# Rows of the strided attention's loads divided at other places, and one weight load divided instead of three

## The chip, the cores and the metric

The kernel runs on one core of one Trainium2 chip. The metric is the device time of one execution in microseconds (us); the median of several runs stands for a kernel. The core has a matrix engine (PE, with its weight loads as PEld), a vector engine (DVE), a scalar engine (ACT), GpSimd (POOL), a sync engine (SP), and sixteen DMA engines that move data between the chip's memory (HBM) and the on-chip memory of 128 partitions (rows). Accumulators lie in PSUM.

## What is computed

Sparse attention, and behind it a mixing layer in the frequency domain:

```
attn: q, k, v (8 batches, 8 heads, 576 positions, 64)
  heads 0-3: a position sees the 32 positions up to itself
  heads 4-7: a position sees earlier positions with the same remainder mod 32
x = attention output as (8, 576, 512)
X = rfft(x over positions), modes 0..63
Yr = Xr @ w_r[m] - Xi @ w_i[m];  Yi = Xr @ w_i[m] + Xi @ w_r[m]   (64 modes, 512 x 512 each)
u = x + irfft(Y);  out = u + relu(u @ w_ch)
```

Inputs are 32-bit. The weights w_r and w_i, 64 matrices of 1 MB each, are by far the most of what is read.

## The kernel before

All inputs are loaded by DMAs that POOL issues, which also make 16-bit numbers of them. POOL issues in program order, so the order of the load calls is the order of the queue.

**Attention, strided heads** (lines 836 to 858). A loop goes over the eight batches. In it `str_scores` and `str_values` work on batch b while `str_front` prepares batch b + 1 by transposing its v, q and k on PE (`str_turn`, line 278; `str_q`, line 262). Each of q, k and v of one batch is a tile of 72 rows (four heads of 18) by 2048 numbers in `ring`, which has twelve places, three for each of four batches. `load_str` (lines 212 to 224) fills them. For batches 0 and 1 it takes 64 rows of one batch at a time (line 222). For an even batch with nb = 2 it takes two batches at once, rows 0 to 63 in one DMA (line 220) and rows 64 to 71 in a second (line 224), for v, then q, then k. These calls come at line 795 for batches 2 and 3, and at line 839 for batches 4 and 5 (issued in the loop at b = 1) and for batches 6 and 7 (at b = 3). With the three of line 224 in the load of batch 0, there are twelve DMAs of 8 rows in all. In memory, a row of a pair of batches is two runs of 2048 numbers, and each run is one DMA packet of 4096 bytes as written.

**Attention, local heads, and the modes** (lines 868 to 888 and 966 to 974). `load_loc` loads 128 rows for each of v, q and k. The modes of one half of the frequencies' input channels are multiplied between the pieces of local attention, those of the other half behind it, with the output projection's preparation in between.

**The weights.** `w_fetch` (lines 159 to 193) loads them in the order of `ORDER`, in tiles numbered i; a tile holds half of one mode's input channels, and one transfer brings a pair of tiles, or four (`QUADS`). Of a transfer the real part goes to partitions 0 to 63 and the imaginary part to 64 to 127, each with a DMA of 64 rows (line 188; line 192 for the last ones, mode by mode). Three real parts, those of the transfers that begin at tiles 64, 84 and 94, are divided by `UNEVEN` into pieces of given numbers of rows, one DMA each (line 185). The weights go round in ten places of `wring` and three guest tiles; `w_fetch` is called when a pair of modes has been multiplied (lines 610 and 657), so POOL waits for PE there.

A tile's semaphore tells when all its DMA has landed, that is, when every DMA engine that took part has written its share. Eight such semaphores go round over POOL's DMAs, so a DMA is issued only when the eighth before it has landed.

**The end** (lines 1134 to 1176). When the last weights have landed, the last two modes are multiplied, and the inverse transform, the projection and the output's rows follow, two batches at a time; SP issues the stores.

Of the kernel before, what the change touches and what calls it, by code (L numbers as in the profile page):

```python
# [56 lines left out]
def kernel(  # L57
# [10 lines left out]
    nc = tc.nc  # L68
# [78 lines left out]
    SPLIT1, SPLIT0 = 56, 48  # L147
    ORDER = [(1, m) for m in range(SPLIT1)] + [(0, m) for m in range(SPLIT0)]
    ORDER += [(1, m) for m in range(SPLIT1, NM)] + [(0, m) for m in range(SPLIT0, NM)]
    UNEVEN = {64: (25, 12, 27), 84: (6, 54, 4), 94: (10, 54)}  # L150
    QUADS = {p for p in range(13, 54) if (p - 13) % 5 in (0, 2)}
    wring = pw.tile([128, 2 * NWBUF, 4, DM], F16, tag="w", bufs=1, name="wring")
    w_tiles = []
# [5 lines left out]
    def w_fetch(n=1):  # L159
        free_pairs[0] += n  # L160
        while len(w_tiles) < 2 * NM:
# [13 lines left out]
            for ri, src in enumerate((moe_w_r, moe_w_i)):  # L175
# [4 lines left out]
                if ri and not m:  # L180
                    dst, rows = dst[:, 1:nm], rows[:, 1:nm]
                if i in UNEVEN and not ri:
                    a = 0
                    for n in UNEVEN[i]:
                        nc.gpsimd.dma_start(dst[a : a + n], rows[a : a + n])
# [24 lines left out]
        return t[:, ds(1152 * vi, 1152)]  # L210

    def load_str(b, nb):
        for vi in (2, 0, 1):
            n = 3 * (b % 4) + SLOT[vi]
            two = ring[:, n : n + 4 : 3, :]
            src = SRC[vi][b - b % 2 : b - b % 2 + 2, 4:8].rearrange(
                "b h (c r) d -> (h c) b (r d)", r=32
            )
            if nb == 2:
                nc.gpsimd.dma_start(two[0:64], src[0:64])  # L220
            else:
                nc.gpsimd.dma_start(ring[0:64, n, :], src[0:64, b % 2])
            if b % 2 == 0:
                nc.gpsimd.dma_start(two[64:72], src[64:72])

    def load_loc(*bs):
        for b in bs:
# [560 lines left out]

    psum_pools(tp=3, sc=3, av=2)
    load_str(0, 1)  # L790
    const_load(nc.scalar, "cI", "cM6", "cM5")
    load_str(1, 1)
    const_load(nc.sync, "cT", "cMl")
    strided_tokens()
    load_str(2, 2)
    w_fetch()

# [212 lines left out]
    for n, i in enumerate([3, 5, 7] + list(range(8, 21))):  # L1010
        b, t = n // 2, n % 2 * 2
# [195 lines left out]
```

## Time and profile before

| what | value |
|---|---|
| median of 3 runs | 423.84 us (423.45 to 425.29) |
| the profiled execution's own time | 423.73 us |
| its span, first to last instruction | 421.7 us |
| PE busy | 327.8 us (78%) |
| DVE, ACT, POOL busy | 236.9, 220.8, 112.2 us (56, 52, 27%) |
| moved by DMA | 91.62 MB in 29914 packets, mean 217 GB/s |
| chain of waits that ended last | DMA 48%, PE 27%, DVE 12%, ACT 6% |

The page of the profile gives the busy time of each engine, the span in 40 equal slices (a digit is the busy share in tenths; for DMA, the mean of the sixteen engines), and the DMA queues with their packets. In the list of the chain of waits, each line has a start, a length and what the time went to; a line of a DMA goes from the end of its issue to its landing. In a timeline, a line has start, length, engine, line of the kernel, operation, output and inputs, shape and count, and in brackets the idle time before it with what ended it. Beneath the page lie the records themselves: every DMA packet with its start, length and size (not with its engine), and for every DMA the sixteen times at which a DMA engine raised its semaphore.

### The profile page before, as it was taken

How to read it: one execution, taken by the hardware profiler on the slowest of the kernel's cores; microseconds unless marked ns; L12 is line 12 of the kernel's file. 1: busy time of each engine (PE TensorE's matmuls, PEld its weight loads, DVE VectorE, ACT ScalarE, POOL GpSimd, SP SyncE). 2: the span in 40 equal slices, each digit the busy share in tenths (PEclk: the TensorE clock that was granted, in tenths of full speed). 3: DMA queues.
4: the chain of work that ended last, by engine and by line, in shares of the span. 5: the costliest groups of instructions: out<-in, count | busy, mean ns of one | idle time of the engine just before them, and what ended most of it. 6: DMA issues, size and time to landing. Idle time of an engine off the chain costs nothing.

```text
span 421.7 us, 9817 instructions
## 1 busy us (share of the span) xinstructions
PE 327.8 (78%) x4156; PEld 201.8 (48%) x4156; DVE 236.9 (56%) x501; ACT 220.8 (52%) x423; POOL 112.2 (27%) x183
## 2 busy tenths in 40 slices
PE   3987878679999198888867858587569748889993
PEld 3866767564656155556534424244235423444320
DVE  3788788950364224555323627756276454665795
ACT  2687778742666157475752513532153345544693
POOL 8332333322422011212031211212112213220594
PEclk9999899956999779899995989999689988999998
DMA  8999999999999999999999999999999999999498
GB/s 149 211 211 212 214 212 213 210 212 210 215 213 213 214 214 214 214 215 214 212 214 214 213 214 214 214 213 213 213 213 215 213 214 214 213 213 182 177 380 341
DMA packets 29914, 91.62 MB, mean 217 GB/s; under 512 B 3952, under 2 KB 4720, under 8 KB 29872
## 3 DMA queue, kind: packets, MB, share of 16 engines
q0 software_dynamic: 24624, 81.28, 97.2%
q1 hardware_dynamic: 4816, 9.65, 6.2%
q8 instruction: 32, 0.52, 0.5%
q10 hardware_dynamic: 432, 0.08, 0.1%
q14 instruction: 10, 0.08, 0.0%
HBM read 162.83 MB, written 9.44 MB: 409 GB/s over the span
## 4 chain that ended last, share of the span: by engine, by line
DMA 48%; PE 27%; DVE 12%; ACT 6%; issue 4%; POOL 1%; DVEq 0%; POOLq 0%; ACTq 0%
DMA wring<-in_moe_w_i_dram 43%; PE y L599 6%; DMA wring<-in_moe_w_r_dram 4%; DVE xb L243 3%; DVE kz L285 3%; PE p L1032 2%; PE sc L534 2%; ACT X L253 2%; PE p L1052 2%; PE sc L461 1%; PE tp L415 1%; ACT PL L491 1%; PE y L534 1%; DVE rec L242 1%; DMA ring<-in_v_dram 1%
## 5 line engine op out<-in xcount | busy, mean ns | idle before, releaser
L599 PE MATMUL y<-wring,X 128*32 128x512 f16 (+1 forms) x424 | 49.1, 454 | 34.5 <-DMA wring<-in_moe_w_i_dram 34.5
L188 POOL DMA_DIRECT2D wring<-in_moe_w_r_dram x39 | 23.7, 607 | 186.4 <-PE y L599 162.5
L253 ACT ACTIVATE yr<-y 128x512 f16<-128x512 f32 x28 | 16.7, 597 | 59.7 <-PE y L599 58.0
L599 PEld LDWEIGHTS <-X 128*32 128x32 f16 (+1 forms) x448 | 21.9, 143 | 48.2 <-DMA wring<-in_moe_w_i_dram 33.0
L751 DVE COPY xo<-tp 128x512 f16<-128x512 f16 x32 | 22.1, 692 | 38.0 <-PE tp L749 38.0
L741 PE MATMUL sc<-w_cp,xT 128*128 128x512 f16 x128 | 37.4, 416 | 1.4 <-DVE xT L709 1.4
L750 ACT ACTIVATE v<-sc 128x512 f16<-128x512 f32 x32 | 19.1, 597 | 36.1 <-PE sc L741 36.1
L243 DVE TENSOR_TENSOR xb<-av,rec 90x256 f16<-90x256 f32 (+2 forms) x80 | 36.0, 450 | 2.7
L491 ACT ACTIVATE PL<-sc 128x480 f16<-128x480 f32 (+1 forms) x48 | 26.9, 578 | 17.2 <-PE sc L477 16.8
L242 DVE RECIPROCAL rec<-av 90x4 f32<-90x4 f32 (+2 forms) x80 | 14.6, 183 | 35.0 <-PE av L506 24.3
L422 DVE COPY qT<-tp 128x576 f16<-128x576 f16 x16 | 11.9, 752 | 37.3 <-PE tp L415 37.3
L1004 DVE TENSOR_TENSOR xo<-p,xo 128x512 f16<-128x512 f32 x32 | 20.6, 686 | 18.2 <-PE p L784 18.2
L188 POOL DMA_DIRECT2D wring<-in_moe_w_i_dram x42 | 25.5, 608 | 9.6 <-DMA wring<-in_moe_w_i_dram 5.3
L380 ACT ACTIVATE PL<-sc 90x360 f16<-90x360 f32 (+1 forms) x48 | 22.8, 490 | 7.0 <-PE sc L373 6.4
L253 ACT ACTIVATE v<-p 128x512 f16<-128x512 f32 x32 | 17.5, 594 | 14.9 <-PE p L784 14.8
L415 PE MATMUL tp<-cI_s,ring 64*64 64x64 f16 x864 | 23.1, 199 | 2.3 <-DVE qT L422 1.7
L253 ACT ACTIVATE v<-tp 128x640 f16<-128x640 f16 (+1 forms) x24 | 19.0, 807 | 10.6 <-PE tp L449 7.9
L461 PE MATMUL sc<-cMl_s,cI_s 128*128 128x480 f16 (+1 forms) x48 | 19.3, 403 | 5.0 <-ACT PL L491 3.4
L415 PEld LDWEIGHTS <-ring 64*64 64x64 f16 x864 | 18.3, 113 | 8.3 <-issue 4.2
L253 ACT ACTIVATE kz<-tp 64x360 f16<-64x360 f16 (+1 forms) x32 | 18.9, 592 | 6.1 <-PE tp L415 5.2
L1090 POOL TENSOR_TENSOR rl<-rl,xo 128x512 f32<-128x512 f32 x15 | 17.1, 1161 | 14.7 <-DVE rl L1083 13.0
L534 PEld LDWEIGHTS <-xb 108*128 108x128 f16 (+2 forms) x176 | 15.4, 106 | 10.8 <-DVE xb L243 6.2
(153 smaller groups left out, 763.1 us busy)
## 6 DMA issues: line engine op xcount, KB each, us to landing
wring<-in_moe_w_r_dram POOLq DMA_DIRECT2D x17, 1024.0 KB, 17.5
wring<-in_moe_w_i_dram POOLq DMA_DIRECT2D x16, 1024.0 KB, 21.8
wring<-in_moe_w_i_dram POOLq DMA_DIRECT2D x24, 512.0 KB, 17.8
wring<-in_moe_w_r_dram POOLq DMA_DIRECT2D x22, 512.0 KB, 14.7
out_dram<-osb SPq DMA_DIRECT2D x18, 256.0 KB, 2.4
out_dram<-osb SPq DMA_DIRECT2D x9, 512.0 KB, 3.3
ring<-in_v_dram POOLq DMA_DIRECT2D x8, 288.0 KB, 13.3
ring<-in_q_dram POOLq DMA_DIRECT2D x8, 288.0 KB, 13.5
```

What stands on the lines that cost most here:

```text
L188: nc.gpsimd.dma_start(dst, rows)
L243: nc.vector.tensor_tensor(out=dst, in0=val.rearrange("p h (q c) -> p h c q", c=4), in1=rec[0:n, 0:pieces] .to_broadcast((n, pieces, 64)) . ...
L253: nc.scalar.activation(out=out, in_=in_, func=ACTF.Copy)
L380: nc.scalar.activation(out=PS[0:n, ds(POFF[t], 4 * n)], in_=scp[0:n, 0 : 4 * n], func=ACTF.Exp, scale=SCALE,)
L415: nc.tensor.transpose(tp[ds(64 * hp, 64), ds(64 * i, 64)], qn[ds(64 * hp, 64), ds(64 * (9 * g + i), 64)], idn[ds(64 * hp, 64), ds(64 * hp, ...
L461: nc.tensor.matmul(scp[:, 0 : n * times].rearrange("p (h x) -> p h x", h=times), idn, mask_rows("cMl", n, times), start=True, stop=False,)
L491: nc.scalar.activation(out=dst, in_=src, func=ACTF.Exp, scale=SCALE)
L534: nc.tensor.matmul(xp[:, ds(192 * cp, 192)].rearrange("p (f m) -> p f m", f=3), xb[b][0:n, base + t, ds(128 * cp, 128)], F[0:n, :, t, :], ...
L599: nc.tensor.matmul(yp[ds(a, 32), :], Xh[half][pr, c].rearrange("p b r (h m) -> p (b r h) m", h=2)[:, :, mm % 32], wt[pr, XC[c], :], start= ...
L741: nc.tensor.matmul(vp, xT[:, ch], w_chs["cp"][:, ch, :], start=(ch == 0), stop=(ch == 3),)
L751: nc.vector.tensor_copy(out=xo.rearrange("p (h q c) -> p h q c", h=2, c=4), in_=tp[:, 0:512].rearrange("p (h c q) -> p h q c", h=2, c=4),)
L1004: nc.vector.tensor_tensor(out=xo[:, j], in0=up[j], in1=xo[:, j], op=AluOp.add)
```

## The change

Two tables of numbers change, and one line uses the new one.

```
-    UNEVEN = {64: (25, 12, 27), 84: (6, 54, 4), 94: (10, 54)}
+    UNEVEN = {64: (3, 40, 21)}
+    CUT = {4: ((54, 18), (20, 52), (24, 48)), 6: ((2, 70), (2, 70), (20, 52))}
...
     def load_str(b, nb):
-        for vi in (2, 0, 1):
+        for j, vi in enumerate((2, 0, 1)):
             n = 3 * (b % 4) + SLOT[vi]
+            cut = CUT[b][j][0] if b in CUT else 64
...
             if nb == 2:
-                nc.gpsimd.dma_start(two[0:64], src[0:64])
+                nc.gpsimd.dma_start(two[0:cut], src[0:cut])
             else:
                 nc.gpsimd.dma_start(ring[0:64, n, :], src[0:64, b % 2])
             if b % 2 == 0:
-                nc.gpsimd.dma_start(two[64:72], src[64:72])
+                nc.gpsimd.dma_start(two[cut:72], src[cut:72])
```

The 72 rows of batches 4 and 5 are divided at row 54 for v, 20 for q and 24 for k, those of batches 6 and 7 at row 2 for v and q and 20 for k; before, all at row 64. Batches 0 to 3 stay as they are. Of the weights, the real part of the transfer at tile 64 goes in pieces of 3, 40 and 21 rows instead of 25, 12 and 27; those at tiles 84 and 94 go in one DMA of 64 rows instead of three and two pieces. The same bytes go to the same places, and POOL issues 152 DMAs instead of 155. The instructions of the other engines, and their order, are the same.

## The prediction

> **What bounds the kernel now.** I read the forty slices first, then the queues, then the end of the chain of waits, and last the trace's single records of DMA packets and landings, which the page only sums up.
>
> ```profile
> DMA  8999999999999999999999999999999999999498
> GB/s 149 211 211 212 214 212 213 210 212 210 215 213 213 214 214 214 214 215 214 212 214 214 213 214 214 214 213 213 213 213 215 213 214 214 213 213 182 177 380 341
> DMA packets 29914, 91.62 MB, mean 217 GB/s; under 512 B 3952, under 2 KB 4720, under 8 KB 29872
> ```
>
> From slice 2 to slice 37 all sixteen DMA engines are busy at one flat rate: loading is the floor from start to 390 us.
>
> ```profile
> q0 software_dynamic: 24624, 81.28, 97.2%
> q1 hardware_dynamic: 4816, 9.65, 6.2%
> q8 instruction: 32, 0.52, 0.5%
> q10 hardware_dynamic: 432, 0.08, 0.1%
> q14 instruction: 10, 0.08, 0.0%
> ```
>
> q0 holds all that POOL issues. q8 is 32 fetches of 16 KB of code; 0.5% of 16 engines' 421.7 us is 33.7 us, so about 1.05 us of one engine each.
>
> ```profile
> 360.96 0.28 issue
> 361.25 19.41 DMA wring<-in_moe_w_i_dram
> 380.66 0.28 issue
> 380.94 9.58 DMA wring<-in_moe_w_i_dram
> 390.52 0.14 issue
> 390.66 0.41 PE y L642 x8
> ```
>
> The last weights land at 390.52; 31.2 us of mixing and output follow, untouched by the change. So the span moves as the last landing does. A transfer has landed only when the slowest of its engines is through: its sixteen landing increments come from 385.44 to 390.52, 5.1 us apart.
>
> **Reading single engines.** On one engine a 4096-byte packet starts 304.5 ns after the one before it, exact to a few ns, and a 4-byte mark (21 ns) ends the engine's part of a transfer. With these steps the records fall into sixteen tracks. On the tracks the pieces of 25, 12 and 27 rows (218 to 220 us) lie so: five engines carry 10 packets of the first, twelve carry 2 of the second, nine carry 6 of the third. One has the first two, four the first and third, five the second and third, six the second alone. So a piece of n rows runs on the largest number up to 16 that divides n, on neighbours, starting behind the last engine of the piece before; 64 rows run on all. The engines left out of a piece get 4-byte fill records, as many as a carrier has packets. That gives 576 fill records here, and 155 POOL transfers x 16 marks + 576 = 3056. The profile's page agrees: 3952 small packets, less 432 of q10 and 464 of q1 (29 transfers x 16).
>
> I number the engines from the one where the count stood at the start; twelve 8-row pieces (96 places) bring it back to 0 before the 25 rows. The code fetches delay eight engines only, 5, 6 and 9 to 14, in that order as far as these groups tell, by about 1.1 us each (one track jumps 1.08 to 1.11 us at each of 332.2, 359.5, 370.2 and 384.6); each has about four by the end. The other eight get none, but the 8 KB fetches of q14 (0.3 to 0.5 us) hit some of 1 to 4.
>
> **The change, step by step.** Bytes are the same; only the engine that carries them changes. Packets of the split transfers (batches 4 to 7 and tiles 64, 84, 94) on each engine, and when its last mark starts, in us; the new end is the old one plus the difference x 0.3045:
>
> | engine | before | after | end before | end after |
> |---|---|---|---|---|
> | 0 | 80 | 86 | 386.67 | 388.50 |
> | 1 to 4 | 84 | 86 | 387.49, 388.44, 388.89, 390.21 | 388.10, 389.05, 389.50, **390.82** |
> | 5, 6 | 76 | 70 | 390.16, 389.49 | 388.33, 387.66 |
> | 7, 8 | 86 | 86 | 388.56, 388.63 | the same |
> | 9 | 76 | 72 | 390.21 | 388.99 |
> | 10, 11 | 72 | 72 | 389.20, 389.06 | the same |
> | 12 | 72 | 70 | 387.84 | 387.23 |
> | 13, 14 | 72 | 70 | 389.48, 389.95 | 388.87, 389.34 |
> | 15 | 72 | 80 | 385.14 | 387.57 |
>
> Three engines tie for last before: 9, 5 and one of 1 to 4, which I call S. The change takes 1.2 and 1.8 us from the first two and gives S two packets more. So the last mark moves from 390.21 to 390.82, **0.61 us later**.
>
> Tiles 84 and 94 lose three POOL issues (8 of L185 become 3, two of L188 come): 3 x 0.6 us on a queue that is 27% busy and waits 162.5 us for PE alone; nothing. No instruction moves past another. Three marks and 32 fill records less: under 0.1 us per engine, taken as nothing.
>
> *S's own stalls* are what the trace does not settle. S loses 0.52 us at 231.4 and again at 344.7, each beside a fetch of q14. If both recur, 390.82. If both fall on engines with room, S ends at 389.77 and the last is about 389.8 (0.4 us earlier than now); with one more, 391.3 (+1.1). I take that they recur, since the instructions around them are the same.
>
> *Earlier arrivals.* The pieces of batches 4 and 5 put 24 packets instead of 18 on engines 0 to 8 by the end of q, so that q lands 1.8 us later on engine 5, which had its fetch at 35.7: about 44.5 instead of 42.73.
>
> ```profile
> 43.39 0.42 PE L262 MATMUL tp<-cI_s,ring 72*128 72x72 f16 x8 [0.84 <-DVE vT L285]
> ```
>
> PE wants it at 43.39, so it waits some 1.1 us. Behind it on PE stand scores and values of batch 3, and the copies of DVE and the exponentials of ACT wait for those: the attention is late by 1.1 us, or by 0 if it catches up. The q of batches 6 and 7, wanted at 61.74, fits within the same delay. What hides it is the full queue. POOL next waits for that work here:
>
> ```profile
> 107.36 0.58 POOL L188 DMA_DIRECT2D wring<-in_moe_w_r_dram  x1 [5.52 <-PE y L599]
> ```
>
> The first packet follows an issue by 1.5 us (1.25 to 2.77 at the start), so it could run at 108.9. S finishes what it has at 111.89, and with 8 packets more at 114.3: 5.4 us of cover. Engines 5, 6 and 12, with 8 packets less, finish near 109.5 and may idle a microsecond; they end 2.5 us or more before S. Cost nothing; without cover, 1 us per 1 us.
>
> [...] From the transfer ahead of the pieces of 25, 12 and 27 rows to the one behind them, the mean landing of the sixteen engines goes from 231.04 to 236.17: 5.13 us for 16 packets on average (4.87 us). So engines left out of a piece do not idle; they go on with what is queued. [...] Taken as if the others idled, the longest parts of all pieces sum to 106 packets after against 108 before, 0.6 us sooner; the landings above disagree with the idling. In the table engines 7 and 15 are not late (388.6 and 385.1). [...]
>
> **Sum.** 423.73 (the profiled execution: span 421.7 and 2.0 around it) + 0.61 = 424.3; the median of the three runs, 423.84, stands 0.1 above that execution. A difference under 0.5% (2.1 us) is what a measurement of this kernel cannot tell from no change.
>
> **Rivals.**
> - *Evener end* (0.28): S's stalls fall elsewhere. Last mark 389.8 to 390.3, time 423.3 to 423.8. For: 9, 5 and 14, the late ones, are all relieved. Against: the fetches come with the program, which is unchanged.
> - *Pieces on the wrong engines* (0.07): slower. If the count stands one or more places off when batch 4 is issued, the extra packets meet engines with fetches. Turning the last column by 1 to 15 places makes the end 2.3 to 4.0 us later than now: 426 to 427.8. It decides from one place on. Against: the six 8-row pieces ahead of it (48 places) are unchanged and bring the count to 0, and this trace shows 0 at 96.
> - *Attention late beyond the cover* (0.02): slower from 5.4 us of delay at 107 on; at 8 us 426.3. The one wait found is 1.1.
> - *Faster by more than 0.5%* (0.03): even sixteen equal ends would come at the mean, 388.71, 1.5 us sooner (0.35%); the rest would have to come from elsewhere.
> - That nothing but total bytes counts (no change, 423.7) lies inside the first.
>
> **Numbers.** Forecast 0.60 (424.1 to 424.9), evener end 0.28, wrong engines 0.07, late attention 0.02, faster 0.03. Within 0.5%: 0.60 + 0.28 = 0.88; slower 0.09; faster 0.03. The range takes in the first two, and 0.3 for the scatter of medians: 423.2 to 425.2.
>
> **What would show it.** POOL transfers 152, small packets 3952 - 48 - 32 = 3872. Last landing 391.1; S last, by 1.3 us over the next; engines 9 and 5 near 389.0 and 388.3. PE waiting for the q load near 43.4. Wrong if another engine is last, if the landing is over 392.6, or if the queue runs empty near 107 us.

## The result and the profile after

The changed kernel takes 438.03 us (median of six runs, 434.84 to 440.62) against 423.7 us before on the same chip: ratio 1.032, interval 1.030 to 1.035. It is slower by 14 us; the forecast was 424.3. Its profiled execution took 434.84 us, with a span of 432.9. It is the quickest of the six, so the trace shows 11.2 of the median's 14.3 us; where the slower runs lose the rest was not traced. The runs scatter more than before (6 us against 2).

The page, as for before (forty slices of 10.8 us; then the packets and the queue that POOL fills):

```profile
DMA  8999999999999999999999999999999999999498
GB/s 153 207 209 179 161 193 145 202 210 209 211 212 212 207 215 214 213 215 217 212 200 215 212 213 215 214 214 215 213 214 215 213 215 213 213 213 189 155 380 340
DMA packets 29834, 91.62 MB, mean 212 GB/s; under 512 B 3872, under 2 KB 4640, under 8 KB 29792
q0 software_dynamic: 24544, 81.28, 98.4%
```

The DMA engines are as busy as before, 9 tenths in nearly every slice of the loading, but from slice 4 to slice 7 they move less: 145 to 193 GB/s where before had 212 to 214. Packets and bytes are as counted beforehand. So the engines do not wait; each packet takes longer. The busy times by stretch show where. Columns: stretch, length, busy us of PE, its weight loads, DVE, ACT and POOL (with instructions), granted clock, DMA share, GB/s. First before, then after:

```profile
38.00:50.00 12.00, 9.87 (x159) 8.43 (x157) 8.93 (x26) 8.94 (x19) 4.05 (x7) 0.86 1.07 213
60.00:76.00 16.00, 13.08 (x237) 11.10 (x234) 13.18 (x37) 12.61 (x29) 5.56 (x10) 1.00 1.07 212
100.00:390.00 290.00, 226.78 (x2765) 131.12 (x2764) 142.47 (x276) 137.98 (x255) 55.15 (x95) 0.91 1.06 213
```

```profile
38.00:50.00 12.00, 5.10 (x69) 4.09 (x68) 5.35 (x13) 4.17 (x10) 2.52 (x5) 0.64 1.19 136
60.00:76.00 16.00, 11.13 (x162) 9.67 (x163) 9.31 (x28) 8.82 (x21) 3.75 (x8) 0.79 1.18 155
100.00:390.00 290.00, 223.76 (x2696) 130.16 (x2691) 138.64 (x271) 137.00 (x254) 55.26 (x97) 0.90 1.07 213
```

The two bad stretches are those of the newly cut rows, batches 4 and 5, then 6 and 7. In the packet records, 4096-byte packets that start between 38 and 50 us took 512 ns in the median, 86% of them over 400; before, 324 ns and 0.3%. (324 ns is the length of a packet's record; an engine's next packet starts 304.5 ns after the one before, so the records overlap a little.) Between 50 and 58 us, when weights pass, the median is 324 again. The last increments of single transfers tell how much is lost by when:

| transfer, its last landing | before | after | later by |
|---|---|---|---|
| last weights ahead of batch 4 | 37.04 | 37.18 | 0.1 |
| k of batches 4 and 5, second piece | 45.63 | 51.96 | 6.3 |
| k of batches 6 and 7, second piece | 63.56 | 75.18 | 11.6 |
| the local k rows that landed at 86 us | 86.08 | 97.05 | 11.0 |
| last weights | 390.52 | 401.68 | 11.2 |

All is lost by 75 us, and nothing more of note afterwards. The chain of waits says so too (start, length, what); its last line is the last landing, and the 31.2 us behind it are as before:

```profile
17.70 14.65 DMA wt<-in_moe_w_i_dram
32.63 19.32 DMA ring<-in_k_dram
52.25 18.52 DMA ring<-in_q_dram
...
392.06 9.62 DMA wring<-in_moe_w_i_dram
```

PE, which in this stretch of before waited mostly for DVE and ACT, now waits for loads. Of what ended PE's waits from 36 to 80 us, this is the top (us in total, times, longest), first before, then after:

```profile
PE av L394 <- ACT PL L380: 3.0, 9, 0.5
PE tp L262 <- DVE vT L285: 1.7, 2, 0.8
```

```profile
PE tp L264 <- DMA ring<-in_q_dram: 6.7, 2, 3.4
PE tp L280 <- DMA ring<-in_v_dram: 3.1, 1, 3.1
```

### The profile page after: what moved, and what is told of

The parts are those of the page before. It is cut to its first block, busy times and chain, and to the rows that moved or that the text cites. A ratio compares the mean times of both kernels' runs of the same rounds, so it can differ in the third digit from the quotient of the medians.

```text
span 432.9 us, 9812 instructions
## 1 busy us (share of the span) xinstructions
PE 329.9 (76%) x4156; PEld 204.4 (47%) x4156; DVE 237.0 (55%) x501; ACT 221.1 (51%) x423; POOL 110.4 (26%) x180
## 2 busy tenths in 40 slices
DMA packets 29834, 91.62 MB, mean 212 GB/s; under 512 B 3872, under 2 KB 4640, under 8 KB 29792
## 3 DMA queue, kind: packets, MB, share of 16 engines
q0 software_dynamic: 24544, 81.28, 98.4%
## 4 chain that ended last, share of the span: by engine, by line
DMA 58%; PE 26%; DVE 7%; ACT 4%; issue 2%; POOL 1%; DVEq 0%; ACTq 0%; POOLq 0%
DMA wring<-in_moe_w_i_dram 43%; PE y L601 7%; DMA ring<-in_k_dram 4%; DMA ring<-in_q_dram 4%; DMA wt<-in_moe_w_i_dram 3%; DMA ring<-in_v_dram 3%; PE tp L417 2%; PE sc L463 2%; PE p L1034 2%; PE y L536 2%; PE p L1054 2%; DVE xb L245 2%; ACT X L255 1%; PE sc L479 1%; ACT PL L493 1%
## 5 line engine op out<-in xcount | busy, mean ns | idle before, releaser
L189 POOL DMA_DIRECT2D wring<-in_moe_w_r_dram x41 | 24.9, 607 | 204.9 <-PE y L601 178.7
L601 PE MATMUL y<-wring,X 128*32 128x512 f16 (+1 forms) x424 | 48.0, 442 | 37.0 <-DMA wring<-in_moe_w_i_dram 36.5
L255 ACT ACTIVATE v<-tp 128x640 f16<-128x640 f16 (+1 forms) x24 | 19.1, 807 | 10.8 <-PE tp L451 7.7
L280 PE MATMUL tp<-cI_s,ring 72*128 72x72 f16 x256 | 15.8, 210 | 7.0 <-DMA ring<-in_v_dram 5.6
```

The costliest lines, as they stand in the source:

```text
L189: nc.gpsimd.dma_start(dst, rows)
L255: nc.scalar.activation(out=out, in_=in_, func=ACTF.Copy)
L601: nc.tensor.matmul(yp[ds(a, 32), :], Xh[half][pr, c].rearrange("p b r (h m) -> p (b r h) m", h=2)[:, :, mm % 32], wt[pr, XC[c], :], start= ...
```

## The experiments

Two theories of why packets got slower. **P**: engines that write at the same time into the same few partitions hold each other up; before, every 64-row transfer would give engine e the rows 4e to 4e+3, whatever the tensor. (The records do not tell which partition a packet goes to; that an engine's rows are neighbours, in the engines' order, is the author's assumption.) **H**: the conflict is in the reading. Rivals of both: the late weight pieces, engines out of step as such, the number of cuts. All compare with before on the same chip.

**1. The late weight pieces alone.**

```
-    CUT = {4: ((54, 18), (20, 52), (24, 48)), 6: ((2, 70), (2, 70), (20, 52))}
+    CUT = {}
```

> The change's other half alone: tile 64's real part in pieces of 3, 40 and 21 rows, tiles 84 and 94 in one transfer each, and all strided rows cut at 64 of 72 as before. Theory A, that the packets of the new strided pieces are slow by themselves (half of those between 38 and 50 us and between 62 and 73 us of the changed kernel took 500 ns or more, where before nearly all took 324): strided loads as before, last landing within 2 us of 390.5, 422 to 426 us, and no packet median over 330 ns between 24 and 80 us. Theory B, that the late weight pieces cost the time: 434 to 440 us.

424.52 us, ratio 1.0014 (1.0005 to 1.0024); last landing 391.03. From 24 to 80 us no slice of its 40 falls below 203 GB/s. So the weight pieces cost 0.6 us, and the rest comes with the strided cuts.

**2 and 3. Batches 4 and 5 alone, batches 6 and 7 alone** (weight pieces as before).

```
+    CUT = {4: ((54, 18), (20, 52), (24, 48))}
...
+    CUT = {6: ((2, 70), (2, 70), (20, 52))}
```

> Only batches 4 and 5 cut at the new rows (54/18, 20/52, 24/48); batches 6 and 7 at 64, weight pieces as before. Theory A: slow packets between 38 and 50 us as in the changed kernel, about 6 us of its 11.2, thus 428 to 432 us, and the rows of batches 6 and 7 at 324 ns again. Theory C, that engines out of step with each other make every strided transfer slow, cut anew or not: batches 6 and 7, which follow engines that are still 4 us apart, are slow too, 433 us or more.

> Only batches 6 and 7 cut at the new rows (2/70, 2/70, 20/52); batches 4 and 5 at 64, weight pieces as before. Theory A: slow packets only from the second piece of 2 rows on, about 5 us lost, 427 to 431 us. If slow packets need what batch 4 left behind (theory C): batches 6 and 7 run mostly at 324 ns and the time is 424 to 426 us.

439.58 us (ratio 1.034, 1.029 to 1.040) and 431.36 (1.017, 1.015 to 1.019). Each is slower than before, and they do not add: the first alone is as slow as both. In the first, packets took 491 ns in the median from 38 to 50 us. The strided rows of batches 6 and 7, cut at 64 there, came mostly at full rate, with one stretch at 58 us down to 162 GB/s; but from 70 to 84 us, where local rows and weights alternate and engines were over 5 us apart, it falls to 148 to 183 GB/s in four slices of 2 us. From 24 to 104 us, in such slices:

```profile
GB/s 209 219 213 213 217 213 209 195 119 139 123 152 168 201 213 213 215 162 193 205 221 203 220 196 148 204 183 171 205 151 193 210 217 212 189 190 190 205 205 210
```

In the second, the median from 58 to 64 us was 574 ns. Expected were 428 to 432 and 427 to 431: the second is missed by 0.4 us, the first by far, because the disturbance outlives the cut rows and because the engines end further apart (see "What the totals hold" below).

**4. Out of step, with the old cut.**

```
-    UNEVEN = {64: (25, 12, 27), 84: (6, 54, 4), 94: (10, 54)}
+    UNEVEN = {64: (25, 12, 27), 84: (6, 54, 4), 94: (10, 54), 0: (54, 10), 2: (20, 44), 4: (24, 40)}
```

> All strided rows cut at 64 as before, but the real parts of the first three weight transfers, just ahead of batch 4, in pieces of the same sizes (54 and 10, 20 and 44, 24 and 40 rows), so that the engines are out of step when batch 4's strided rows come. Theory A with the cause in the strided source or in rows above 64: weight packets stay at 324 ns, strided ones too, 423 to 427 us (the balance at the end moves). Theory C: batch 4's strided packets are slow though they are cut as before, 428 us or more. If pieces of any tensor are slow: the weight packets themselves between 24 and 37 us are at 400 ns or more.

436.64 us, ratio 1.029 (1.025 to 1.033). Its rate from 20 to 60 us, in slices of 1 us:

```profile
GB/s 205 193 156 127 209 160 148 213 213 217 188 201 213 217 205 213 209 193 205 217 209 217 209 213 213 209 217 213 209 217 225 205 209 213 217 213 209 209 221 213
```

The weight pieces themselves are slow (127 to 160 GB/s in four of the five slices from 22 to 27 us; 67% of the packets from 22 to 24 us over 400 ns), so neither the strided tensor nor rows above 64 are needed for it. Later pieces of the same weights, of 20, 44, 24 and 40 rows, pass with 6% of the packets from 28 to 38 us over 400 ns: uneven pieces are not always slow. And from 38 to 50 us the strided rows, cut at 64, pass at 324 ns with their landings 6 us apart: being out of step does no harm there, where every transfer gives the same engine the same partitions by the assumption above. The rate falls again later (181 to 189 GB/s in five slices of 2 us between 74 and 96 us), where the local loads of 128 rows, eight to an engine, meet weights. "Out of step as such" falls.

**5. The cost by itself.** In the kernel before, batch 4's strided loads give way to three equal readings with different targets (the rows of batches 4 and 5 that the attention needs are left out, and fewer bytes move, so the total time tells nothing; the same holds for 8, 10 and 11).

```
+            if b == 4:
+                six = SRC[vi][2:8, 4:8].rearrange(
+                    "b h (c r) d -> (h c) b (r d)", r=32
+                )[0:16]
+                to = (slice(0, 16), slice(16, 80, 4), slice(80, 96))[j]
+                nc.gpsimd.dma_start(ring[to, 0:6, :], six)
+                continue
```

> The disputed cost by itself. Batch 4's strided loads (whose results are then not the attention's) are replaced by three transfers that read alike, 16 rows of six batches of v, q and k, one row for each of the 16 engines and six packets of 4096 B for each: v's go to partitions 0 to 15, q's to every fourth partition from 16 to 76, k's to partitions 80 to 95. Theory P, that engines which write into the same few groups of partitions hold each other up: v's and k's packets take twice the 324 ns or more, q's take 324. Theory H, that the conflict lies in the reading (or in the number of engines): all three take the same. [...] The total time is of no use here, since fewer bytes move.

The three transfers, then the weights behind them:

```profile
36.60:39.00 2.40, 1.79 (x37) 1.43 (x34) 2.00 (x7) 2.37 (x6) 0.04 (x1) 1.00 1.18 114
39.90:40.90 1.00, 0.38 (x6) 0.22 (x5) 0.97 (x3) 0.95 (x3) 0.00 (x0) 1.00 1.06 205
41.40:43.00 1.60, 0.00 (x0) 0.00 (x0) 0.67 (x3) 0.00 (x0) 0.57 (x1) 0.62 1.19 113
44.00:46.00 2.00, 1.81 (x25) 1.63 (x26) 0.62 (x2) 0.65 (x2) 0.58 (x1) 0.50 1.08 217
```

16 engines into 16 neighbouring partitions: 114 GB/s, median packet 664 ns. The same reading into every fourth partition: 205 GB/s, 324 ns. Into 16 neighbours again: 113 GB/s, 677 ns. But for the tensor, the only difference is where it is written, and the two slow tensors stand on either side of the quick one; P holds, and H cannot account for it. An undisturbed engine moves 4096 bytes in 304.5 ns, 13.5 GB/s; an estimate from these rows is that 16 neighbouring partitions take what 114 / 13.5 = 8.4 engines move at full pace, about one engine to two partitions.

**6. Other sources, same targets.** Kernel 4, with every second row of all eight heads read in place of every row of four.

```
+            if b in (4, 6):
+                src = SRC[vi][b : b + 2, 0:8].rearrange(
+                    "b h (c r) d -> (h c) b (r d)", r=32
+                )[0:144:2]
```

> The kernel with the early weight pieces (54/10, 20/44, 24/40), in which the engines were 6 us apart and the strided rows still took 324 ns a packet, with one edit: the strided rows of batches 4 to 7 are read from every second 8 KB row of all eight heads in place of every row of four heads (other data, so the results differ), while the partitions written and the engines stay. Theory P: strided packets stay at 324 ns between 38 and 50 us and the time within 3 us of 436.6. Theory H: the engine no longer reads the block that the other transfers' rule gives it, so the strided packets take 400 ns or more between 38 and 50 us, and the time is 440 us or more.

436.88 us against kernel 4's 436.64; from 38 to 50 us the packets still take 324 ns. H falls.

**7. The changed kernel with q's rows moved to other partitions.**

```
+            if b in CUT and vi == 0:
+                two = two[56:128]
```

> The changed kernel with one edit: q's strided rows of batches 4 to 7 are written to partitions 56 to 127 in place of 0 to 71 (the attention then works on old q rows); cuts, sources, engines and bytes are unchanged. Theory P: q's pieces mostly leave the partitions that v's and k's use, fewer engines meet on one group, and between 38 and 50 us more than the changed kernel's 130 GB/s moves, 160 or more; 429 to 435 us. Theory H: the same slow packets, 435 to 440 us.

431.05 us, ratio 1.020 (1.016 to 1.026): half of the 14 us is gone with nothing but a third of the targets moved. Rates from 24 to 80 us in slices of 1.4 us, the changed kernel and then this one:

```profile
GB/s 208 222 199 217 217 205 214 219 205 222 182 135 132 123 117 97 176 135 164 208 202 225 208 217 214 167 176 184 176 141 140 102 132 176 100 178 201 189 181 206
```

```profile
GB/s 208 214 217 205 222 208 222 199 225 205 211 211 173 214 196 140 155 211 211 211 217 214 196 143 126 179 217 199 217 170 123 169 203 215 197 205 212 208 205 209
```

The first bad stretch shrinks to three short dips (190 GB/s over 38 to 50 us against 136). What is left may be v's and k's pieces, which still share partitions; that was not tried. (The attention here reads older q rows.)

**8. Eight engines, and those beside them.** Two transfers of 8 rows, on the two halves of the engines: v to partitions 0 to 7, q to 72, 76, ... 100.

```
+                )[0:8]
+                to = (slice(0, 8), slice(72, 104, 4))[j % 2]
```

> How few engines suffice, and whether they hold up others. Batch 4's strided loads (whose results are then not the attention's) are replaced by two transfers of 8 rows of six batches, six packets of 4096 B on each of 8 engines: v's to partitions 0 to 7, q's to every fourth partition from 72 to 100; k's are left out. The two use different engines and run side by side. [...] If engines on a crowded group hold up those elsewhere too, q's packets are slow while v's run. [...] The total time is of no use, since fewer bytes move.

```profile
35.00:36.00 1.00, 0.72 (x15) 0.66 (x15) 0.97 (x4) 0.23 (x1) 0.54 (x1) 1.00 1.11 217
36.40:38.00 1.60, 1.35 (x23) 1.26 (x23) 0.95 (x4) 0.68 (x3) 0.00 (x0) 1.00 1.29 136
39.20:40.20 1.00, 0.78 (x20) 0.60 (x16) 0.64 (x3) 1.00 (x2) 0.05 (x1) 1.00 1.09 213
```

From 36.4 to 38 us all 49 packets that start, on whichever engine, took 400 ns or more (median 587). By their targets only v's eight engines crowd; the others wrote weights to partitions 64 to 127 and q's scattered rows, and were slowed as well. As q's rows lie among the weights' partitions, some crowding between these two at the same moments is not excluded; at 39.2 us, when v is nearly through, q and the next weights run at 324 ns.

**9. A single cut**, v's rows of batches 4 and 5.

```
+    CUT = {4: ((54, 18), (64, 8), (64, 8))}
```

> The kernel before with a single new cut: v's rows of batches 4 and 5 at 54 of 72; all else as before. Theory P: slow packets for some 5 us about 40 us, where 54 and 18 rows meet q's 64, and again where the engines, now up to 3 us apart, carry the last rows of one kind of transfer and the first of another (72 to 100 us, local rows and weights in turn): 426 to 431 us. If slow packets came from the number of new cuts, a sixth of the change's 14 us: 424 to 426.5.

431.21 us, ratio 1.019 (1.015 to 1.023), 0.2 us above what P was given: one cut of six costs half of the whole, so the number of cuts does not set the price. From 24 to 104 us, slices of 2 us:

```profile
GB/s 209 215 215 211 213 215 213 160 137 195 211 211 213 209 219 207 225 203 215 211 215 211 182 198 219 188 201 158 191 209 210 219 174 216 171 186 209 209 217 205
```

Slow at 38 to 42 us; at full rate from 44 to 66 us, though landings are 3.6 to 4.1 us apart; slow again at 68 to 94 us (158 at 78), where two kinds of transfer alternate. Experiments 2 and 4 show such a tail too.

**10 and 11. How wide is a group?** v to every second partition from 0 to 14; q, beside it, to every second one from 16 to 30, and in the other kernel from 32 to 46.

```
+                to = (slice(0, 16, 2), slice(16, 32, 2))[j % 2]
...
+                to = (slice(0, 16, 2), slice(32, 48, 2))[j % 2]
```

> How wide a group is, and whether two groups 32 partitions apart are one. Batch 4's strided loads (whose results are then not the attention's) are replaced by two transfers of 8 rows of six batches, on the two halves of the engines, side by side, to every second partition: v's to 0, 2, ... 14, q's to 16, 18, ... 30. Groups of four partitions, each with two engines: all 96 packets at 324 ns. Groups of eight partitions or more, with four engines: 500 ns and more, as in the transfer of 8 rows to partitions 0 to 7. The total time is of no use, since fewer bytes move.

> The kernel with v's rows on partitions 0, 2, ... 14 and q's on 16, 18, ... 30, with q's moved to 32, 34, ... 46 and nothing else. If partitions 32 apart share the limit, four engines meet on each of four groups: packets of both transfers at 500 ns or more while both run, and all engines slow with them. If they don't, 324 ns as with q's at 16. [...]

```profile
36.50:38.50 2.00, 1.78 (x38) 1.54 (x36) 1.80 (x6) 1.94 (x6) 0.57 (x1) 1.00 1.06 207
38.50:40.50 2.00, 1.54 (x30) 1.19 (x30) 1.72 (x4) 1.90 (x4) 1.15 (x2) 1.00 1.06 215
```

```profile
36.50:38.50 2.00, 1.69 (x35) 1.33 (x32) 1.61 (x7) 1.96 (x5) 0.00 (x0) 1.00 1.34 131
38.50:40.50 2.00, 1.21 (x20) 0.84 (x20) 1.90 (x5) 1.85 (x5) 0.57 (x1) 1.00 1.08 115
```

Eight engines on partitions 0 to 14 in steps of two run at 324 ns, where eight on 0 to 7 did not (median 587 in experiment 8). That fits groups of four partitions that take two engines, and as well groups of eight that take four: the runs do not tell the two apart. In either case one engine to two partitions kept full pace. Moving q by 16 partitions more, from 16 to 32, takes the rate from 207 and 215 GB/s to 131 and 115 (median 720 ns from 36.7 to 39 us). So partitions 0 to 14 and 32 to 46, 32 apart, share here what neighbours share.

**What the totals hold.** The time follows the last of the sixteen engines, so a total mixes two losses: all engines later, by slow packets, and one engine further behind the others, by an uneven share of packets, which is what the prediction's table counts. The sixteen increments of the last landing tell them apart. Columns, from the profiled executions: the last increment later than before; the mean of the sixteen later than before; the last one behind this mean (1.5 us in before); and the mean later at the weights that land at 90 us in before.

| kernel | last | mean | last behind mean | mean, at 90 us |
|---|---|---|---|---|
| changed | 11.2 | 10.7 | 2.0 | 10.0 |
| 2, batches 4 and 5 | 16.4 | 12.5 | 5.4 | 7.8 |
| 3, batches 6 and 7 | 7.4 | 5.1 | 3.8 | 4.7 |
| 4, early weights | 12.7 | 9.0 | 5.2 | 3.5 |
| 7, q moved | 5.8 | 5.2 | 2.1 | 4.8 |
| 9, one cut | 6.7 | 5.3 | 2.9 | 4.2 |

So experiments 2 and 4 owe almost 4 us each to uneven shares (the table's count of packets gives 4.2 and 5.4), of which the whole change has little, and they go on losing after 90 us: in experiment 2, 39% of the packets from 290 to 300 us took over 400 ns, at 173 GB/s against 213 before. Which transfers meet there was not looked into. On the mean, too, halves do not add (12.5 and 5.1 against 10.7), and one cut costs half.

## Why the prediction was wrong, point by point

- *The bound* was right: the last landing moves by 11.2 us, the span by 11.2, and the tail stays at 31.2.
- *Which engine carries what* was right as far as it can be seen: 152 transfers, 3872 small packets, 24544 in q0, to the packet. The sixteen last landings lie 3.9 us apart (5.1 before; 3.6 in the table), so the balancing itself came about. But the last of them is 0.4 us after the next, not 1.3, and which engine it is the records do not tell.
- *The step that failed* is "the new end is the old one plus the difference x 0.3045". It took the 304.5 ns, "exact to a few ns", as the price of a packet on any engine and in any piece, so that it summed to 0.61 us; the landing moved by 11.2. In the changed kernel the median packet record took 512 ns from 38 to 50 us and 471 from 60 to 76, against 324. Experiments 5, 8, 10 and 11 show 324 ns with at most one engine to two partitions, where those 32 apart are counted together, and medians of 587 to 720 ns with one to each partition. A 64-row transfer keeps to the first by itself, if rows are shared out in order: an engine has four rows to itself, and if all rows 32 apart share as those of experiment 11 did, it meets one other engine there, always the same, for all strided and real-part loads. 54, 20, 24, 2 or 70 rows would then give the same engines other rows, and pieces of neighbouring transfers, running side by side, can meet in the same partitions. That they do so in the changed kernel is inferred; experiment 7 supports it by moving targets alone.
- *What the trace of before could show.* It has uneven pieces too, the eight of the late weights with 384 packets, and they kept 324 ns (0.5% of the packets from 278 to 310 us over 400). So the price looked safe for any piece. One difference is that between two such weight transfers stands a part for partitions 64 to 127, while v's, q's and k's pieces all go to 0 to 71; that this decides was not tried.
- *Where pieces do not crowd, the table held.* The same count of packets for experiment 1 puts the last mark at 391.17 (engine 14, with four packets more: 389.95 + 4 x 0.3045) instead of 390.21, 0.96 us later; the last landing came 0.5 us later and the profiled time 0.6. In the changed kernel the lag grows only from 11.0 to 11.2 us between 97 us and the end.
- *Earlier arrivals* were mis-sized by the same step: q of batches 4 and 5 lands at 48.45, not 44.5, and PE waits 3.1 us for v and up to 3.4 for q instead of 1.1. That this delay costs nothing of its own fits the trace: loading goes on at 213 GB/s from 100 us on, as before, and the queue does not run empty.
- *The rivals*: "pieces on the wrong engines" had the sign, at 426 to 427.8 us; crowding was not among them, and the range ended at 425.2. By the prediction's own sign, a landing over 392.6, it was wrong: 401.7.

Open: why the 8-row pieces of before, two packets each for eight engines into partitions 64 to 71, keep 324 ns. The sixteen landings of such a transfer lie up to 2.1 us apart, so that few of its packets may meet; that was not tried. Nor do the runs give a rule for how much a given pair of pieces loses, or a price for a crowd between one engine to two partitions and one to each.

## What to carry to other kernels

Before dividing a transfer anew, write down which engine writes which partitions, for this transfer and for the ones that run beside it, and count the engines on a stretch of neighbouring partitions together with those on the stretch 32 further on: one engine to two partitions kept full pace here (205 to 215 GB/s in experiments 5 and 10), one to each slowed all loading (113 to 136 GB/s in 5, 8 and 11), and what lies between was not tried. A packet time that is constant in a profile was measured for that pattern of targets: 324 ns before, 512 in the median from 38 to 50 us with other targets. Engines that are merely out of step cost nothing in experiments 4 and 9 while transfers of one layout followed each other (324 ns with landings 6 us apart; 203 to 225 GB/s with landings 3.6 to 4.1 us apart); packets got slower where loads of 128 and of 64 rows alternated (down to 181 and 158 GB/s).

## What the runs showed of the hardware that was not expected

- 16 engines into 16 neighbouring partitions move 113 and 114 GB/s, into every fourth partition 205 (experiment 5).
- Crowded partitions slowed the engines that write elsewhere, too: all 49 packets in 1.6 us at 400 ns or more, with eight of sixteen engines in the crowd (experiment 8, with the reserve stated there). Why is open.
- Engines on partitions 0 to 14 and 32 to 46 crowd each other, engines on 0 to 14 and 16 to 30 do not: 131 and 115 against 207 and 215 GB/s (experiments 11 and 10).
